# Eighteen groups of transposes in a three-stage fp32 kernel go by 16-bit halves and a transposing DMA instead of by TensorE

## Chip, cores and metric

One core of one Trainium2 chip runs the whole program. The metric is the device time of one execution in microseconds (us), the median of several executions. Before the change it is 501.43 us (three executions, 501.25 to 501.67).

## What is computed

The reference is a chain of three layers on activations of 2 batches x 768 tokens x 512 features, all in fp32:

```python
x = attention(q, k, v)                 # 8 heads of 64, a band of 96 keys and 8 global keys
xt = x.transpose(0, 2, 1)              # first mixer
h = np.maximum(xt @ w_tok1, 0.0) @ w_tok2
u = x + h.transpose(0, 2, 1)
x = u + np.maximum(u @ w_ch1, 0.0) @ w_ch2
theta = x @ w_theta                    # second mixer
zr, zi = x * np.cos(theta), x * np.sin(theta)
y = einsum('ts,bsd->btd', w_tok_r, zr) + einsum('ts,bsd->btd', w_tok_i, zi)
u = x + y
out = u + np.maximum(u @ w_ch, 0.0)
```

The weights arrive as 64-bit floats and are turned into fp32 on the chip.

## The kernel before, in words

**Numbers.** An fp32 matrix product is made of three products of shorter numbers: each operand is split into a high part (hi) and the rest (lo), and `mm3` (line 90) issues hi x hi, hi x lo and lo x hi. ScalarE (ACT) writes hi, VectorE (DVE) or GpSimd (POOL) writes lo = value - hi. `evac_split` (line 704) does that with a result of TensorE (PE) in PSUM.

**Layout.** `x[b]` holds a batch by rows: 6 blocks `s` of 128 tokens on the partitions, 512 features along a partition. A product over features needs the features on the partitions, so each block has to be turned. `turn_rows` (line 775) does that: four PE transposes of 128x128 (line 779) into a PSUM tile, then `evac_split`, so ACT writes hi and DVE lo, both from PSUM. It is called for 24 groups: six `ut` of batch 0, six `ut` of batch 1 (operands of the channel product of the first mixer, kept in `ut[b]`), and twelve `xt`, one for each of the 12 blocks of both batches (operands of `theta` in the second mixer).

**Stages.** Attention of both batches, with the token mixing of batch 0 woven in, takes until about 115 us. `token_mix2` (line 985) does the rows of batch 1 and turns three of its blocks; the other three are turned in the first steps of `channel_mix` (line 996). That has 24 steps (b, k) of 12 per batch. In a step `up` of the step after is issued (8 times 3 products of 512 and of 256 columns into two PSUM banks with the tag "t"; `evac_split` gives the tile `g`), then `down` of the step itself (18 products, tile `h2`). In the steps of batch 1 a small dictionary, `plan`, puts the beginning of the second mixer between `up` and `down`: `pb.turn`, `pb.theta` and `pb.rotate` of the first blocks.

**Second mixer.** `PhaseB.run` (line 1241) goes through 12 steps, one for each block i = (b, s). In step i it issues, in this order: `mix(i, 0)` (24 products of 256 columns), `rotate(i + 1)`, `turn(i + 3)`, `theta(i + 2)`, `mix(i, 1)`, one tick, `mix(i, 2)` (12 products of 512 columns each), and in the first four steps a second tick. From step 7 on parts of the last product (`last`, tile `v`) are put between.
- `theta` (line 1088): 12 products on PE, then five DVE instructions (lines 1105 to 1113) and three of ACT (lines 1116 to 1118) for sine and cosine. `w` for blocks 0 and 1 lies in the pool `tp`, for the others in the pool of `g`.
- `rotate` (line 1129): two DVE products (line 1136), two ACT copies (hi, line 1137), two POOL subtractions (lo, line 1139), and one POOL addition (line 1143) that writes the turned block back into `x`. `z` is what `mix` of the next step reads.
- `turn` (line 1082): `turn_rows` into one of four `xt` tiles, three of the pool `xt` and one in a part of a `z` tile.

**Weights.** Weights are converted by jobs, which run a phase at each tick (`tick`, line 181): load (DMA issued by SyncE, SP), `job_scale` (two ACT), `job_join` (two DVE, lines 145 and 148, and one POOL addition, line 149), `job_high` (one ACT, line 157), `job_low` (one DVE, line 160). One job begins at each tick at most, so several are under way in different phases. In `channel_mix` of batch 0 there are two ticks a step, in that of batch 1 one in `up` and one after `down` where k is not in `plan`.

**What sets the order.** The order is written out by hand. Every engine takes its instructions in the order in which the program issues them, and SP its DMAs as well; an instruction that waits holds back those behind it on its engine.

Of the kernel before, what the change touches and what calls it, by code (L numbers as in the profile page):

```python
# [15 lines left out]
F32 = mybir.dt.float32  # L16
F32R = mybir.dt.float32r
I32 = mybir.dt.int32
U16 = mybir.dt.uint16
AF = mybir.ActivationFunctionType  # L20
ALU = mybir.AluOpType
# [4 lines left out]
P = 128  # L26
NS = S // P
NHP = H // 2
E = H * D
NE = E // P  # L30
# [3 lines left out]
NF = DCH // P  # L34
# [12 lines left out]
LAG = 3  # L47
# [13 lines left out]
def f(ap):  # L61
    return ap.bitcast(F32)


def r(ap):
    return ap.bitcast(F32R)
# [17 lines left out]
class Build:  # L84
# [326 lines left out]
    def attention_band(self, pairs_pool, first, h1):  # L411
# [6 lines left out]
        with tc.tile_pool(name="au", bufs=2) as up, tc.tile_pool(name="aa", bufs=2) as ap:  # L418
# [142 lines left out]
            for u in range(N + 2):  # L561
# [22 lines left out]
                if not turned:  # L584
                    between()
                self.run_steps(
                    turn(u - 1, start and u < N - 4, between) if turned else [],
                    values(u - 2) if 0 <= u - 2 < N else [],
                )
# [180 lines left out]
    def turn_row(self, tag, b, s):  # L770
        h, s0 = divmod(s * P, E)
        hi, lo = (t[h][:, :, s0 : s0 + P] for t in self.ut[b])
        self.turn_rows(tag, self.x[b][:, s, :], r(hi), r(lo), "ut_%d_%d" % (b, s))

    def turn_rows(self, tag, src, hi, lo, name):

        pt = self.ps.tile([P, NE, P], F32, name=name, tag=tag)
        for d in range(NE):
            self.nc.tensor.transpose(pt[:, d, :], src[:, d * P : (d + 1) * P], self.ident)  # L779
        self.evac_split(hi, lo, pt)  # L780
# [192 lines left out]
    def moe(self, es, a8s, w12p, h1):  # L973
        tc = self.tc
        ws = es.enter_context(tc.tile_pool(name="ws", bufs=1, side="right"))
        self.moe_jobs(ws, w12p)
        self.prefetch()
        pend = self.token_mix2(h1)
        a8s.close()
        gp = es.enter_context(tc.tile_pool(name="g", bufs=2, side="right"))  # L980
        xtp = es.enter_context(tc.tile_pool(name="xt", bufs=3, side="right"))
        tp = es.enter_context(tc.tile_pool(name="tb", bufs=1, side="right"))
        self.channel_mix(gp, PhaseB(self, xtp, tp, gp), pend)

    def token_mix2(self, h1):
        pend = []
        for s in range(NS):
            self.token_row("acc", h1, 1, s)
            pend.append(s)
            if len(pend) > LAG:  # L990
                self.turn_row("t", 1, pend.pop(0))
            if s % 2:
                self.tick()
        return pend

    def channel_mix(self, gp, pb, pend):
        nc = self.nc
        steps = [(b, k) for b in range(B) for k in range(NF)]
        ho = {}

        def up(b, k):
            self.need(self.wc_job[k, 0])
            c1 = self.wc[k][0]
            uth, utl = self.ut[b]
            g = gp.tile([P, 2, S], F32R, name="g_%d_%d" % (b, k), tag="g")
            for h, hs in enumerate((slice(0, E), slice(E, S))):
                ps = self.ps.tile([P, hs.stop - hs.start], F32, name="gp_%d_%d_%d" % (b, k, h), tag="t")
                self.mm3(
                    ps,
                    [  # L1010
                        ((r(c1[0][:, d]), r(c1[1][:, d])), (r(uth[h][:, d]), r(utl[h][:, d])))
                        for d in range(NE)
                    ],
                )
                self.evac_split(g[:, 0, hs], g[:, 1, hs], ps, relu=True)
                if pend:
                    self.turn_row("acc", 1, pend.pop(0))
                if b == 0 or h == 1:
                    self.tick()
            return g  # L1020

        def down(b, k, g):
            self.need(self.wc_job[k, 1])
            c2 = self.wc[k][1]
            if k == 0:
                ho[b] = [
                    self.ps.tile([P, E], F32, name="h2_%d_%d" % (b, s), tag="acc") for s in range(NS)
                ]
            for s in range(NS):
                cs = slice(s * P, (s + 1) * P)  # L1030
                self.mm3(
                    ho[b][s],
                    [((g[:, 0, cs], g[:, 1, cs]), (r(c2[0]), r(c2[1])))],
                    first=k == 0,
                    last=k == NF - 1,
                )
                if k == NF - 1:
                    x = self.x[b][:, s, :]
                    nc.vector.tensor_tensor(out=x, in0=ho[b][s], in1=x, op=ALU.add)

        g = up(*steps[0])
        plan = {4: [(pb.turn, 0)], 5: [(pb.theta, 0)], 6: [(pb.rotate, 0), (pb.turn, 1)],
                7: [(pb.theta, 1)], 9: [(pb.turn, 2)]}
        for i, (b, k) in enumerate(steps):
            nxt = up(*steps[i + 1]) if i + 1 < len(steps) else None
            if b == 1:
                for act, n in plan.get(k, ()):
                    act(n)
            down(b, k, g)
            if b == 1 and k < NF - 1 and k not in plan:  # L1050
                self.tick()
            if (b, k) == (0, NF - 2) or b == 1:
                self.gate += 1
            g = nxt
        pb.run()


class PhaseB:
# [10 lines left out]
        self.todo = [(b, s) for b in range(B) for s in range(NS)]  # L1069
        self.xt, self.z, self.y, self.u3 = {}, {}, {}, {}  # L1070

    def xtbuf(self, i):
        j = i % 4
        if j not in self.xtile:
            if j < 3:
                self.xtile[j] = self.xtp.tile([P, 2, NE, P], F32, name="xt%d" % j, tag="xt")
            else:
                t = self.ztile[1][:, 4:6]
                self.xtile[j] = t.rearrange("p l (d x) -> p l d x", d=NE)
        return self.xtile[j]  # L1080

    def turn(self, i):
        b, s = self.todo[i]
        t = self.xt[i] = self.xtbuf(i)
        x = self.k.x[b][:, s, :]
        self.k.turn_rows("t", x, r(t[:, 0]), r(t[:, 1]), "xt_%d_%dp" % (b, s))

    def theta(self, i):
        K, nc = self.k, self.k.nc
# [151 lines left out]
    def run(self):  # L1241
        K = self.k
        n = len(self.todo)
        TA, TB = self.TA, self.TB
        ends = []
        for b in range(B):
            ends += [(b, 0, (0, 1), 0, TB), (b, 0, (2, 3), 0, TB)]
            ends += [(b, 1, (d,), 0, TA) for d in range(NE)]
        ends[-1:] = [(1, 1, (NE - 1,), c, c + TB) for c in range(0, TA, TB)]
        for i, (b, s) in enumerate(self.todo):  # L1250
            self.mix(i, 0)
            if i + 1 < n:
                self.rotate(i + 1)
            if i + 3 < n:
                self.turn(i + 3)
            if i + 2 < n:
                self.theta(i + 2)
            if b == 1 and s in (0, NS - 1):
                self.last_split(s // (NS - 1), 0)
            self.mix(i, 1)  # L1260
            if b == 1 and s > 0:
                self.last(*ends[s - 1])
            if b == 1 and s == 2:
                self.last_split(0, 1)
            K.tick()
            self.mix(i, 2)
            if i < 4:
                K.tick()
        self.last_split(1, 1)
        for end in ends[NS - 1 :]:  # L1270
            self.last(*end)
# [54 lines left out]
```

## Time and profile before

| | |
|---|---|
| median of 3 executions | 501.43 us |
| the profiled execution | 501.55 us, its span 499.8 us |
| PE busy | 494.2 us (99%) |
| DVE busy | 309.0 us (62%) |
| ACT busy | 235.7 us (47%) |
| POOL busy | 163.5 us (33%) |
| TensorE clock granted | 1.0 of full speed in all 40 slices |
| DMA | 45.93 MB, mean 92 GB/s |

The span runs from the first to the last instruction; the 1.75 us between it and the time of the execution lie around it. The duration that the profile gives for a matmul includes its way through the pipeline, so that durations of neighbours overlap; what a matmul costs PE is read from the starts, or from the chain of work that ended last, where the pieces of PE stand end to end.

### The profile page before, as it was taken

The page shows a single profiled execution, that of the slowest core. Times are in us where ns is not written, and L with a number is a line of the kernel's source. Part 1 is how long each engine was busy: PE and PEld are TensorE (multiplying, and loading weights), DVE is VectorE, ACT ScalarE, POOL GpSimd, SP SyncE. Part 2 cuts the span into 40 slices and gives each one's busy share as a digit, 9 for nine tenths or more (in the row PEclk, how much of TensorE's full clock was granted, in tenths as well). Part 3 has the DMA queues.
Part 4 walks back from the last instruction along what each step waited for, and adds up shares of the span by engine and source line. Part 5 has one row for each costly group of instructions (what it writes and reads, how often), then busy time and mean ns, then how long its engine had stood idle before and what let it go on. Part 6 is the DMA issues. An engine that isn't in the chain of part 4 may idle for free.

```text
span 499.8 us, 7723 instructions
## 1 busy us (share of the span) xinstructions
PE 494.2 (99%) x2908; PEld 420.2 (84%) x2908; DVE 309.0 (62%) x671; ACT 235.7 (47%) x458; POOL 163.5 (33%) x175
## 2 busy tenths in 40 slices
PE   9999999999999999999999999999999999999997
PEld 4888878887888888888888888888888889888896
DVE  4788878836876675206573566387888785451342
ACT  6888778714755454112554444445555434232010
POOL 7355444410342323001332151244555543333000
PEclk9999999999999999999999999999999999999999
DMA  6697764201453443002343122222210000000012
GB/s 200 202 266 246 229 215 141 87 2 50 142 159 127 134 126 114 0 1 55 119 129 121 42 54 73 85 85 65 84 64 1 1 1 0 22 22 22 21 66 104
DMA packets 30013, 45.93 MB, mean 92 GB/s; under 512 B 1936, under 2 KB 20880, under 8 KB 29968
## 3 DMA queue, kind: packets, MB, share of 16 engines
q1 hardware_dynamic: 29968, 45.36, 29.7%
q8 instruction: 25, 0.41, 0.3%
q14 instruction: 20, 0.16, 0.1%
HBM read 42.21 MB, written 3.15 MB: 91 GB/s over the span
## 4 chain that ended last, share of the span: by engine, by line
PE 98%; ACT 1%; issue 0%; DVE 0%; DVEq 0%
PE gp L96 20%; PE y L96 20%; PE h L96 20%; PE th L96 7%; PE v L96 7%; PE mm L96 7%; PE o L406 6%; PE s L437 5%; PE t L484 5%; PE warm L330 1%; PE ut L779 1%; PE xt_0p L779 0%; PE xt_2p L779 0%; PE xt_1p L779 0%; ACT e L578 0%; PE xt_4p L779 0%
## 5 line engine op out<-in xcount | busy, mean ns | idle before, releaser
L149 POOL TENSOR_TENSOR cvt<-cvt,cvs 128x512 int32<-128x512 int32 (+1 forms) x57 | 75.8, 1330 | 217.5 <-DVE cvt L148 171.2
L96 PE MATMUL h<-wc,g 128*128 128x512 f32 x432 | 102.1, 390 | 0.0
L96 PE MATMUL gp<-xh,wc 128*128 128x512 f32 (+1 forms) x384 | 97.6, 336 | 0.0
L96 PEld LDWEIGHTS h<-wc,g 128*128 128x128 f32 x432 | 79.6, 188 | 15.4
L708 DVE SCALAR_TENSOR_TENSOR g<-gp,g 128x512 fp32r<-128x512 f32 (+1 forms) x48 | 26.7, 557 | 83.9 <-ACT g L706 83.9
L96 PEld LDWEIGHTS gp<-xh,wc 128*128 128x128 f32 x384 | 67.2, 189 | 8.6 <-DVE xl L712 0.2
L96 PE MATMUL gp<-xl,wc 128*128 128x512 f32 (+1 forms) x192 | 64.3, 335 | 0.0
L706 ACT ACTIVATE g<-gp 128x512 fp32r<-128x512 f32 (+1 forms) x48 | 23.5, 490 | 70.5 <-PE gp L96 70.5
L96 PE MATMUL y<-wri,z 128*128 128x256 f32 (+1 forms) x288 | 51.9, 335 | 0.0
L96 PE MATMUL y<-wri,s 128*128 128x256 f32 (+1 forms) x288 | 51.8, 335 | 0.0
L96 PEld LDWEIGHTS y<-wri,s 128*128 128x128 f32 x288 | 44.7, 189 | 5.9
L96 PEld LDWEIGHTS y<-wri,z 128*128 128x128 f32 x288 | 44.6, 188 | 6.0
L484 PE MATMUL t<-ident,e 128*128 128x128 f32 x176 | 48.0, 285 | 0.4 <-ACT at L496 0.4
L145 DVE SCALAR_TENSOR_TENSOR cvs<-cvt,cvs 128x512 int32<-128x512 int32 (+1 forms) x57 | 44.3, 777 | 0.0
L96 PEld LDWEIGHTS gp<-xl,wc 128*128 128x128 f32 x192 | 36.0, 188 | 4.5
L484 PEld LDWEIGHTS t<-ident,e 128*128 128x128 f32 x176 | 31.7, 184 | 8.1 <-issue 2.0
L450 DVE CUSTOM_DVE_ANT_0 e<-s,base 128x256 f32<-128x256 f32 (+1 forms) x96 | 32.8, 398 | 8.6 <-PE s L437 7.9
L139 ACT ACTIVATE cvt<-raw 128x512 f32<-128x512 f32 (+1 forms) x57 | 37.2, 653 | 2.0 <-issue 2.0
L140 ACT ACTIVATE cvs<-raw 128x512 int32<-128x512 uint16 (+1 forms) x57 | 37.3, 654 | 0.0
L1116 ACT ACTIVATE w<-w 128x512 f32<-128x512 f32 x12 | 7.6, 633 | 56.9 <-DVE w L1113 56.9
L406 PE MATMUL o<-v,at 128*128 128x65 f32 x192 | 32.3, 252 | 0.0
L406 PEld LDWEIGHTS o<-v,at 128*128 128x128 f32 x192 | 29.8, 196 | 0.0
(136 smaller groups left out, 812.9 us busy)
## 6 DMA issues: line engine op xcount, KB each, us to landing
raw<-w_ch SPq DMA_DIRECT2D x28, 512.0 KB, 3.6
raw<-w_tok SPq DMA_DIRECT2D x21, 512.0 KB, 3.6
k<-k SPq DMA_DIRECT2D x7, 480.0 KB, 5.5
v<-v SPq DMA_DIRECT2D x8, 384.0 KB, 3.9
out<-o SPq DMA_DIRECT2D x11, 256.0 KB, 2.0
q<-q SPq DMA_DIRECT2D x7, 384.0 KB, 4.9
raw<-w_theta SPq DMA_DIRECT2D x4, 512.0 KB, 3.6
a<-v SPq DMA_DIRECT2D x8, 240.0 KB, 4.7
```

The source lines that it names most:

```text
L96: self.nc.tensor.matmul(out, lhsT=a, rhs=b, start=first and i == 0, stop=last and i == n - 1)
L139: nc.scalar.activation(out=f(t), in_=f(top), func=AF.Copy, scale=2.0**-111)
L140: nc.scalar.activation(out=s, in_=nxt, func=AF.Copy, scale=2.0**-13)
L145: nc.vector.scalar_tensor_tensor(out=s, in0=t, scalar=-(1 << 31), in1=s, op0=ALU.bitwise_and, op1=ALU.bitwise_or)
L149: nc.gpsimd.tensor_tensor(out=t, in0=t, in1=s, op=ALU.add)
L406: self.nc.tensor.matmul(po[:, j * OW : j * OW + D + 1], lhsT=at, rhs=v[:, j * (D + 1) : (j + 1) * (D + 1)], start=first, stop=last,)
L437: nc.tensor.matmul(ps[j][:, ii, c0:], lhsT=t["q"][pj, i * P : (i + 1) * P], rhs=kf[pj, i * KW - P + c0 : i * KW + P], start=True, stop=True,)
L450: nc.vector.tensor_tensor_reduce(out=e, in0=ps[j][:, ii, c0:], in1=self.base[2 * hp + j][min(i, 1)], op0=ALU.add, op1=ALU.min, scale=-SCAL ...
L484: nc.tensor.transpose(pt[:, ii, c, :], e[j][:, ii, c * P : (c + 1) * P], self.ident)
L706: nc.scalar.activation(out=hi, in_=ps, func=AF.Relu if relu else AF.Copy)
L708: nc.vector.scalar_tensor_tensor(out=lo, in0=ps, scalar=0.0, in1=f(hi), op0=ALU.max, op1=ALU.subtract)
L1116: nc.scalar.activation(out=a, in_=t, func=AF.Abs)
```

## The change

All groups of transposes but the six of batch 0 leave PE. A block of `x` (128 partitions x 512 fp32) is seen as 1024 16-bit halves per partition. `halves_out` copies them so that all lower halves come first and then all upper halves, and SP issues one transposing DMA from SBUF to SBUF (eight blocks of 128x128 halves). `halves_join` copies the turned halves back into their pairs, which gives the turned fp32 block. `halves_split` writes hi (ACT) and lo (DVE), both from SBUF.

For the six blocks of `ut[1]` the two copies are on POOL, in steps k = 2 to 9 of batch 0 of `channel_mix`, issued between `up` and `down`: a block goes out in step s + 2, is joined in step s + 3 and split in step s + 4. For the twelve `xt` blocks the two copies are on ACT; the first four go out in steps of `plan` and the others in `run`, where a step now issues `mix(i, 0)`, `rotate(i + 1)`, `turn_in(i + 3)`, `turn_out(i + 4)`, `theta(i + 2)` and so on. Blocks going out share one tile ("cut") with one buffer; there are three `xt` tiles, the third in the place of `w` of blocks 0 and 1. Steps k = 4 and k = 9 of batch 1 get a tick that they did not have.

```diff
+    def halves_out(self, src, t, copy):
+        a = t[:, 1].rearrange("p d x -> p (d x)").bitcast(U16)
+        b = t[:, 0].rearrange("p d x -> p (d x)").bitcast(U16)
+        copy(
+            out=a.rearrange("p (w n) -> p w n", w=2),
+            in_=src.bitcast(U16).rearrange("p (n w) -> p w n", w=2),
+        )
+        self.nc.sync.dma_start_transpose(out=b.rearrange("p (m x) -> p m x", x=P), in_=a)
+    def halves_join(self, t, copy):
+        b = t[:, 0].rearrange("p d x -> p (d x)").bitcast(U16)
+        c = t[:, 1].rearrange("p d x -> p (d x)").bitcast(U16)
+        copy(out=c.rearrange("p (n w) -> p w n", w=2), in_=b.rearrange("p (w n) -> p w n", w=2))
+    def halves_split(self, t, hi, lo):
+        self.nc.scalar.copy(out=hi, in_=t[:, 1])
+        self.nc.vector.tensor_tensor(out=lo, in0=t[:, 1], in1=f(hi), op=ALU.subtract)
...
-        xtp = es.enter_context(tc.tile_pool(name="xt", bufs=3, side="right"))
+        xtp = es.enter_context(tc.tile_pool(name="xt", bufs=1, side="right"))
...
     def token_mix2(self, h1):
-        pend = []
         for s in range(NS):
             self.token_row("acc", h1, 1, s)
-            pend.append(s)
-            if len(pend) > LAG:
-                self.turn_row("t", 1, pend.pop(0))
             if s % 2:
                 self.tick()
-        return pend
+    def columns_out(self, pb, s):
+        t = self.turning[s] = pb.scratch("ut_%d" % s, ("cut", "xt0", "xt1")[s % 3])
+        self.halves_out(self.x[1][:, s, :], t, self.nc.gpsimd.tensor_copy)
+    def columns_split(self, s):
+        h, s0 = divmod(s * P, E)
+        hi, lo = (u[h][:, :, s0 : s0 + P] for u in self.ut[1])
+        self.halves_split(self.turning.pop(s), r(hi), r(lo))
...
-                if pend:
-                    self.turn_row("acc", 1, pend.pop(0))
...
-        plan = {4: [(pb.turn, 0)], 5: [(pb.theta, 0)], 6: [(pb.rotate, 0), (pb.turn, 1)],
-                7: [(pb.theta, 1)], 9: [(pb.turn, 2)]}
+        self.turning = {}
+        plan = {2: [(pb.turn_out, 0)], 3: [(pb.turn_in, 0), (pb.turn_out, 1)], 4: [(pb.turn_in, 1)],
+                5: [(pb.theta, 0)], 6: [(pb.rotate, 0), (pb.turn_out, 2)], 7: [(pb.theta, 1)],
+                8: [(pb.turn_in, 2)], 9: [(pb.turn_out, 3)]}
         for i, (b, k) in enumerate(steps):
             nxt = up(*steps[i + 1]) if i + 1 < len(steps) else None
+            if b == 0:
+                if 0 <= k - 4 < NS:
+                    self.columns_split(k - 4)
+                if 0 <= k - 3 < NS:
+                    self.halves_join(self.turning[k - 3], nc.gpsimd.tensor_copy)
+                if 0 <= k - 2 < NS:
+                    self.columns_out(pb, k - 2)
...
-            if b == 1 and k < NF - 1 and k not in plan:
+            if b == 1 and k < NF - 1 and k not in (5, 6, 7):
                 self.tick()
...
-    def xtbuf(self, i):
...
-    def turn(self, i):
...
+    def scratch(self, n, tag="cut"):
+        return self.xtp.tile([P, 2, NE, P], F32, name="cut_" + n, tag=tag, bufs=1)
+    def turn_out(self, i):
+        b, s = self.todo[i]
+        t = self.cut = self.scratch("xt_%d_%d" % (b, s))
+        self.k.halves_out(self.k.x[b][:, s, :], t, self.k.nc.scalar.copy)
+    def turn_in(self, i):
+        K = self.k
+        j = (2, 1, 0)[i % 3] if i > 2 else i % 2
         if j not in self.xtile:
+            pool, tag = (self.tp, "t") if j == 2 else (self.xtp, "xt%d" % j)
+            self.xtile[j] = pool.tile([P, 2, NE, P], F32, name="xt%d" % j, tag=tag)
+        t = self.xt[i] = self.xtile[j]
+        K.halves_join(self.cut, K.nc.scalar.copy)
+        K.halves_split(self.cut, r(t[:, 0]), r(t[:, 1]))
...
             if i + 3 < n:
-                self.turn(i + 3)
+                self.turn_in(i + 3)
+            if i + 4 < n:
+                self.turn_out(i + 4)
             if i + 2 < n:
                 self.theta(i + 2)
```

## Rows read from the trace of the kernel before

**Rows 1.** The page: the chain that ended last, shares of the span by engine.

```profile
PE 98%; ACT 1%; issue 0%; DVE 0%; DVEq 0%
```

**Rows 2.** The chain that ended last, in order of time: start us, us, what.

```profile
266.76 0.66 PE xt_0p L779 x4
...
335.28 0.44 PE xt_3p L779 x4
335.71 2.77 PE th L96 x12
...
444.24 2.72 PE th L96 x12
```

**Rows 3.** PE in order of time: start us, us, line and operation, idle before.

```profile
128.34 0.60 PE L779 MATMUL ut<-ident,x 128*128 128x128 f32 x4
128.70 0.37 PE L96 MATMUL gp<-xh,wc 128*128 128x256 f32 x1
```

**Rows 4.** POOL in order of time, steps 3 and 4: lo parts of z, one x.

```profile
373.93 3.00 POOL L1139 TENSOR_TENSOR s<-w,s 128x512 fp32r<-128x512 f32 x2
376.88 1.30 POOL L1143 TENSOR_TENSOR x<-xt 128x512 f32<-128x512 f32 x1
...
386.84 3.01 POOL L1139 TENSOR_TENSOR z<-w,z 128x512 fp32r<-128x512 f32 x2
```

**Rows 5.** PE in order of time: mix part 0 of steps 4 and 5.

```profile
378.18 2.99 PE L96 MATMUL y<-wri,s 128*128 128x256 f32 x24
...
389.65 3.02 PE L96 MATMUL y<-wri,z 128*128 128x256 f32 x24
```

**Rows 6.** DVE in order of time, second mixer, with idle time and its releaser.

```profile
363.39 0.68 DVE L1105 TENSOR_SCALAR w<-th 128x512 f32<-128x512 f32 x1
...
372.13 2.38 DVE L1136 TENSOR_TENSOR w<-x,w 128x512 f32<-128x512 f32 x2
375.69 0.69 DVE L712 TENSOR_TENSOR xt<-xt_0p,xt 128x512 fp32r<-128x512 f32 x1 [1.18 <-ACT xt L706]
376.30 0.68 DVE L1105 TENSOR_SCALAR w<-th 128x512 f32<-128x512 f32 x1
377.02 1.44 DVE L1108 TENSOR_SCALAR w<-w 128x512 f32<-128x512 f32 x1
...
399.33 0.68 DVE L1105 TENSOR_SCALAR w<-th 128x512 f32<-128x512 f32 x1
405.69 1.28 DVE L1136 TENSOR_TENSOR w<-x,w 128x512 f32<-128x512 f32 x2
408.76 0.68 DVE L1105 TENSOR_SCALAR w<-th 128x512 f32<-128x512 f32 x1
```

**Rows 7.** ACT in order of time, step 3 of the second mixer.

```profile
374.55 0.62 ACT L1137 CAST s<-w 128x512 fp32r<-128x512 f32 x1 [1.02 <-DVE w L1136]
375.07 0.59 ACT L706 ACTIVATE xt<-xt_0p 128x512 fp32r<-128x512 f32 x1
```

**Rows 8.** Groups of instructions by line and shape: count, busy us, mean ns.

```profile
L779 PE MATMUL ut<-ident,x 128*128 128x128 f32 x48 | 7.0, 272 | 0.0
L379 POOL TENSOR_SCALAR xh<-x 128x256 fp32r<-128x256 f32 x24 | 11.3, 472 | 29.5 <-DVE x L399 29.5
L1204 ACT CAST u<-x 128x1024 fp32r<-128x1024 f32 x2 | 2.0, 1040 | 0.0
L145 DVE SCALAR_TENSOR_TENSOR cvs<-cvt,cvs 128x512 int32<-128x512 int32 x53 | 41.7, 787 | 0.0
```

**Rows 9.** POOL in order of time, one step of channel_mix, batch 0.

```profile
156.57 1.29 POOL L149 TENSOR_TENSOR cvt<-cvt,cvs 128x512 int32<-128x512 int32 x1 [1.76 <-DVE cvt L148]
161.74 1.29 POOL L149 TENSOR_TENSOR cvt<-cvt,cvs 128x512 int32<-128x512 int32 x1 [3.88 <-DVE cvt L148]
```

**Rows 10.** DMA issues: KB each, median us from issue to landing.

```profile
out<-o SPq DMA_DIRECT2D x11, 256.0 KB, 2.0
raw<-w_tok SPq DMA_DIRECT2D x4, 384.0 KB, 7.3
```

More of the change, by code (lines that the diff above doesn't have):

```diff
@@ L977, in moe, with channel_mix @@
         self.prefetch()
-        pend = self.token_mix2(h1)
+        self.token_mix2(h1)
         a8s.close()
         gp = es.enter_context(tc.tile_pool(name="g", bufs=2, side="right"))
-        xtp = es.enter_context(tc.tile_pool(name="xt", bufs=3, side="right"))
+        xtp = es.enter_context(tc.tile_pool(name="xt", bufs=1, side="right"))
         tp = es.enter_context(tc.tile_pool(name="tb", bufs=1, side="right"))
-        self.channel_mix(gp, PhaseB(self, xtp, tp, gp), pend)
+        self.channel_mix(gp, PhaseB(self, xtp, tp, gp))
     def token_mix2(self, h1):
-        pend = []
         for s in range(NS):
             self.token_row("acc", h1, 1, s)
-            pend.append(s)
-            if len(pend) > LAG:
-                self.turn_row("t", 1, pend.pop(0))
             if s % 2:
                 self.tick()
-        return pend
-    def channel_mix(self, gp, pb, pend):
+    def columns_out(self, pb, s):
[5 more added lines that the diff above has]
+        self.halves_split(self.turning.pop(s), r(hi), r(lo))
+    def channel_mix(self, gp, pb):
         nc = self.nc
@@ L1070, in __init__ @@
         self.xt, self.z, self.y, self.u3 = {}, {}, {}, {}
-    def xtbuf(self, i):
-        j = i % 4
-        if j not in self.xtile:
[L1075 to L1080, printed above, removed]
-    def turn(self, i):
[L1083 to L1086, printed above, removed]
+    def scratch(self, n, tag="cut"):
[7 more added lines that the diff above has]
+        j = (2, 1, 0)[i % 3] if i > 2 else i % 2
+        if j not in self.xtile:
+            pool, tag = (self.tp, "t") if j == 2 else (self.xtp, "xt%d" % j)
[3 more added lines that the diff above has]
+        K.halves_split(self.cut, r(t[:, 0]), r(t[:, 1]))
     def theta(self, i):
```

## The prediction

> **What bounds the kernel now.** I read the chain of work that ended last first. TensorE holds 98% of it [rows 1], so any time taken from PE's queue is gained, as long as no other engine takes its place. The chain in order of time tells what PE pays for a group of four transposes: 0.66 us in the steps of batch 1 of the channel product, 0.44 us in the second mixer [rows 2]. The starts in PE's timeline say the same of `ut`: 128.70 - 128.34 = 0.36 us [rows 3].
>
> Then I looked for the engine that comes next, by asking when `z` is ready and when `mix` wants it. Step 4: POOL ends at 373.93 + 3.00 = 376.93 [rows 4], PE begins at 378.18 [rows 5], 1.25 us to spare. Step 5: 386.84 + 3.01 = 389.85 against 389.65, nothing to spare; PE's 24 products took 3.02 us instead of 2.99, for the lo parts come third. The reason is DVE: from one `theta` to the next its queue takes 376.30 - 363.39 = 12.91 us where two ticks' jobs stand in a step [rows 6], while PE's step takes 389.65 - 378.18 = 11.47 us [rows 5]. DVE falls behind by 1.44 us a step and just reaches step 5 when the jobs run out; without them its turn is 408.76 - 399.33 = 9.43 us [rows 6]. So the second mixer is bound by PE with DVE close behind it, and that decides what the change keeps.
>
> **The sum, part by part.**
>
> *Transposes that leave PE.* Six `ut`: 6 x 0.36 = 2.2 us [rows 3]. Three `xt` in channel steps: 3 x 0.66 = 2.0 us; the part over 0.44 there is a wait for a PSUM bank of the tag "t", which goes too, since `down` needs none. Nine in `run`: 9 x 0.44, and `theta` behind them takes 2.77 instead of 2.72 us [rows 2], so 9 x 0.49 = 4.4 us. Together 8.6 us.
>
> The mean duration of one `ut` transpose is 272 ns in the groups [rows 8], and four of them begin within 0.36 us [rows 3], so I take the starts. The Trainium skill, page "TensorE: Matmul & The Clock Gate", Part 4, gives a transpose 390 ns alone and about 275 ns in a kernel. The row's duration agrees with the latter. Were that what PE pays, 72 transposes would be 72 x 0.275 = 19.8 us and the time 485 us; by the starts it is not.
>
> *Batch 0 of the channel product.* A step (8.2 us) gets two POOL copies of 1024 halves, one ACT copy, one DVE subtraction, one DMA. No row shows a copy of halves on POOL. From the nearest rows: one with a single input takes 472 ns for 256 elements [rows 8], so 1.3 to 1.9 us for 1024 by the share that is fixed; one with two inputs 1.29 us for 512 [rows 9], 2.6 us. I take 1.5, a single input. POOL's idle time in a step is 1.76 + 3.88 = 5.64 us [rows 9]: 3.0 us fit, and 5.2 just fit. Cost nothing, covered by POOL waiting for DVE. If the cover is gone, the additions of line 149 come late, ACT's line 157 behind them, and so the evacuation of `g`. Weights are finished three ticks, 1.5 steps, ahead of their use, which absorbs a few us. `ut` of block 5 is split in step 9 and read from step 11's `up` on.
>
> *Batch 1's channel steps.* Four copies out and three joins on ACT, each near 1.04 us (1024 elements, [rows 8]): 7 us over eight steps of 8.2 us, with ACT at less than half. Nothing, covered by ACT waiting for PE. The two added ticks move two jobs forward, out of `run`.
>
> *The DMA.* No transposing DMA is in the trace. Bounds by rows: 256 KB out land in 2.0 us, the slowest loads, 384 KB, in 7.3 us [rows 10]; I take 4, since it queues behind loads of weights. SP issues it behind loads whose buffers are released by earlier work, so it starts when the copy out ends. In `run` it has the rest of the step: a step less join, hi, lo and copy out (1.04 + 0.6 + 0.7 + 1.04 = 3.4), 11.0 - 3.4 = 7.6 us. Nothing within the bounds.
>
> *The turn in `run`.* Here it costs. Before, ACT writes hi right behind its second copy of `z` (375.07, [rows 7]) and DVE waits 1.18 us for it [rows 6]. Now the join stands before hi: about 1.04 us more. lo would begin at 375.07 + 1.04 + 0.6 = 376.7 instead of 375.69. Its source was PSUM and is now SBUF, so it has two inputs in SBUF, and such an instruction is held while POOL works: the two products of line 1136 take 2.38 us beside POOL and 1.28 without, and line 1108 ends at 377.02 + 1.44 = 378.46, just behind POOL's addition (376.88 + 1.30 = 378.18) [rows 4, 6]. lo arrives near the end of the second subtraction (376.93). If it gets in before the addition, it ends near 377.5, line 1108 then finds POOL done, and the turn is 0.25 us longer. If the addition goes first, lo ends near 378.75, and the turn is 1.4 us longer. I take 0.9, the middle, since lo arrives within 0.2 us of the edge. ACT's copy out waits for lo and then runs beside `theta`'s 4 us on DVE. In step 0 hi also waits for `w`, whose place the third tile takes; `theta` waits for PE there anyway, I estimate 0.3 us.
>
> *What is late next.* PE's step is 0.49 us shorter, DVE's turn 0.9 longer. `z` of step 4: 1.25 - 4 x 0.49 - (0.3 + 2 x 0.9) + 0.3 (the lo parts come third) = -2.5 us. `z` of step 5: -0.2 - 5 x 0.49 - (0.3 + 3 x 0.9) + 0.3, and + 1.9 for the job that is gone from the step before (line 145's 0.79 [rows 8], and products that no longer meet POOL, 2.38 - 1.28): -3.4 us. So PE waits 2.5 us in step 4 and 0.9 more in step 5. With 0.25 it is 1.5 us in all, with 1.4 it is 5.0. After that a turn without jobs is 9.43 + 1.4 at most, under 10.98, and nothing more is lost.
>
> *Sum.* 501.55 - 8.6 + 3.4 = 496.35 us for the profiled execution, which lies 0.12 above the median: **496.2 us**.
>
> **Rivals.**
> 1. *All hidden.* lo finds its gap, and the two jobs moved forward relieve the early steps. For it: DVE has 9.43 us turns later. Against it: nothing is to spare in step 5 now. 501.4 - 8.6 = 492.8 us. Chance 0.14.
> 2. *DVE's turn grows by more than 1.4 us.* ACT's strided copies or the wait for the copy out are longer than 1.04 us; then turns without jobs also exceed PE's 10.98 us, and DVE bounds the second mixer. At 2 us: -0.2 - 2.45 - 6.3 + 0.3 + 1.9 = 6.8 us lost: 499.6 us. For it: no row shows ACT reading or writing every second half at this width. Against it: a turn without jobs has 1.5 us to spare. Chance 0.18.
> 3. *POOL is too slow in batch 0.* At 2.6 us a copy, and DVE held meanwhile, the joins of weights and the two copies follow each other in about 10.9 us against 8.2 over six steps, 16 us, less some 12 of lead: 4 us, with the 3.4: 500 us, up to 503. Against it: single inputs. Chance 0.08.
> 4. *The transposing DMA is slow* (other side). Its blocks go one after another. Place: the join in `run`, in front of `theta`'s ACT work and of lo on DVE. It decides from about 7.6 us: each us over that is paid in about six steps of 11 us. A transposition as slow as the slowest load, behind a load of half that, takes 7.3 + 3.6 = 10.9 us: 6 x 3.3 = 20 less 3 to spare, 501.4 - 8.6 + 17 = 510 us. Against it: 256 KB in 2.0 us [rows 10] and idle queues after the last loads. Chance 0.10. The Trainium skill, page "VectorE: DVE Perf Modes", "The three transpose paths", gives 1309 ns for one 128x128 block by the DMA's crossbar. Eight blocks in a row would be 10.5 us, near this case; no run here shows it yet.
>
> **How the numbers follow.** My case has 0.50, 494.4 to 498 us by its bounds. A difference under 0.2% (1 us) can't be told from none here. Faster: my case, rival 1, most of rival 2 and a little of rival 3: 0.82. Same: ends of rivals 2 and 3, 0.07. Slower: rival 4 and an end of rival 3, 0.11. The range 492.4 to 500.8 takes in rivals 1 and 2 and leaves out rival 4 and most of rival 3.
>
> **What would show it.** Right: no transposes on PE after 121 us; the first `mix` of steps 4 and 5 preceded by PE idle that POOL's line 1139 ends, 3 us in all; lo before 1105 of DVE beginning 1 us later after the products; `theta`'s turn near 13.8 us in steps 1 and 2. Wrong: ACT's join waiting for a DMA (rival 4), POOL without idle time before 200 us (rival 3), PE idle in steps 6 to 11 (rival 2), none at all (rival 1), or PE waiting in the channel steps, which I cost at nothing.

## The result, and the profile after

497.38 us, median of four executions (496.91 to 497.50), against 501.43 of four as well: a ratio of 0.9917, 95% interval 0.9900 to 0.9934. The forecast was 496.2 us, range 492.4 to 500.8. The profiled execution took 497.50 us with a span of 495.7 us, 4.1 us less than before. Line numbers above 775 have moved: the copy out is 779, the transposing DMA 783, the join 789, hi and lo of a turned block 792 and 793, `theta` 1139 to 1152, `rotate` 1170 to 1177; in some of the runs below they lie a few lines off these.

The page of the changed kernel: busy time, the granted clock by slices, the chain by engine.

```profile
PE 486.2 (98%) x2836; PEld 413.8 (83%) x2836; DVE 312.6 (63%) x671; ACT 264.8 (53%) x482; POOL 180.8 (36%) x187
PEclk9999999999999999999999999999998999999999
PE 84%; DVE 7%; ACT 4%; DMA 2%; POOL 1%; SPq 1%; issue 1%; DVEq 0%; ACTq 0%; POOLq 0%
```

PE still has most of the chain [rows 1], but DVE, ACT and POOL now have parts of it, and one slice shows a lower clock. Where this lies is seen in PE's timeline of the second mixer (start, duration, idle before and what ended it), the first part of `mix` in steps 1 to 5 and `theta` of step 4:

```profile
338.64 2.99 PE L96 MATMUL y<-wri,z 128*128 128x256 f32 x24
...
349.63 2.99 PE L96 MATMUL y<-wri,s 128*128 128x256 f32 x24
...
360.62 3.15 PE L96 MATMUL y<-wri,z 128*128 128x256 f32 x24
...
373.46 0.50 PE L96 MATMUL y<-wri,s 128*128 128x256 f32 x2 [1.52 <-ACT s L1171]
375.17 4.38 PE L96 MATMUL y<-wri,s 128*128 128x256 f32 x22 [1.20 <-POOL s L1173]
379.38 2.93 PE L96 MATMUL th<-s,xt 128*128 128x512 f32 x12
...
387.58 2.99 PE L96 MATMUL y<-wri,z 128*128 128x256 f32 x24
```

A step takes 349.63 - 338.64 = 10.99 us instead of 11.47 [rows 5]. Step 4 was due at 360.62 + 10.99 = 371.61, which is 378.18 - 371.61 = 6.6 us earlier than before [rows 5]. It then waits for the hi and the lo parts of `z`, and its 24 products end 4.9 us late: `theta` begins at 379.38, due at 371.61 + 2.83 = 374.44. No later step waits for `z`. The five groups of transposes still to come then give 5 x 0.49 = 2.4 us: 6.6 + 2.4 = 9.0 gained, 4.9 given back, 4.1 left.

DVE in step 2 and its neighbours, with the idle time before an instruction and what ended it:

```profile
348.40 0.68 DVE L1139 TENSOR_SCALAR w<-th 128x512 f32<-128x512 f32 x1
...
356.13 2.39 DVE L1170 TENSOR_TENSOR w<-x,w 128x512 f32<-128x512 f32 x2
361.19 1.53 DVE L793 TENSOR_TENSOR xt<-cut_xt,xt 128x512 fp32r<-128x512 f32 x1 [2.67 <-ACT xt L792]
362.65 0.68 DVE L1139 TENSOR_SCALAR w<-th 128x512 f32<-128x512 f32 x1
363.36 0.43 DVE L1142 TENSOR_SCALAR w<-w 128x512 f32<-128x512 f32 x1
```

ACT in the same step:

```profile
358.55 0.62 ACT L1171 CAST z<-w 128x512 fp32r<-128x512 f32 x1 [1.03 <-DVE w L1170]
359.08 1.36 ACT L789 COPY cut_xt<-cut_xt 128x1024 uint16<-128x1024 uint16 x1
360.47 0.62 ACT L792 CAST xt<-cut_xt 128x512 fp32r<-128x512 f32 x1
```

POOL in steps 2 to 4:

```profile
357.93 3.00 POOL L1173 TENSOR_TENSOR z<-w,z 128x512 fp32r<-128x512 f32 x2
360.90 1.27 POOL L1177 TENSOR_TENSOR x<-xt 128x512 f32<-128x512 f32 x1
...
372.17 2.94 POOL L1173 TENSOR_TENSOR s<-w,s 128x512 fp32r<-128x512 f32 x2
...
384.97 2.55 POOL L1173 TENSOR_TENSOR z<-w,z 128x512 fp32r<-128x512 f32 x2 [2.00 <-issue]
```

DVE's turn from `theta` to `theta` is 362.65 - 348.40 = 14.25 us, 1.34 us more than before [rows 6]. Read together: ACT writes the second hi of `z`, then the join (1.36 us), then hi of the turned block. lo reaches the head of DVE's queue at 361.19, 0.29 us after POOL has begun its addition (360.90), and takes 1.53 us instead of 0.69 [rows 6]: it ends 0.55 us behind the addition's end (362.17). Line 1142, which stood behind that addition before (1.44 us, [rows 6]), now takes 0.43 us. The Trainium skill, page "SBUF — State Buffer", section "SBUF: two separate sides", says that a DVE instruction with two SBUF inputs and a GpSimd instruction that reads SBUF take one port pair by turns, for a whole instruction. This timeline agrees: of lo's 1.53 us, 0.98 pass beside the addition, and it ends 0.55 us behind it.

`z` of step 4 is finished by POOL at 372.17 + 2.94 = 375.11, 3.5 us after PE wanted to begin.

The new copies (groups by line and shape) and the transposing DMAs (SP's issues, median us from issue to landing):

```profile
L789 ACT COPY cut_xt<-cut_xt 128x1024 uint16<-128x1024 uint16 x12 | 16.3, 1362 | 0.0
L779 ACT COPY cut_xt<-x 128x1024 uint16<-128x1024 uint16 x12 | 12.5, 1046 | 10.0 <-DVE xt L793 10.0
L789 POOL COPY cut_ut<-cut_ut 128x1024 uint16<-128x1024 uint16 x6 | 9.6, 1594 | 2.9 <-DMA cut_ut<-cut_ut 2.9
L779 POOL COPY cut_ut<-x 128x1024 uint16<-128x1024 uint16 x6 | 7.6, 1262 | 0.0
```

```profile
cut_xt<-cut_xt SPq DMA_TRANSPOSE x12, 2.7
cut_ut<-cut_ut SPq DMA_TRANSPOSE x6, 2.7
```

### The profile page after: what moved, and what is told of

It reads as the page before. It is cut to its first block, busy times and chain, and to the rows that moved or that the text cites. A ratio compares the mean times of both kernels' runs of the same rounds, so it can differ in the third digit from the quotient of the medians.

```text
span 495.7 us, 7653 instructions
## 1 busy us (share of the span) xinstructions
PE 486.2 (98%) x2836; PEld 413.8 (83%) x2836; DVE 312.6 (63%) x671; ACT 264.8 (53%) x482; POOL 180.8 (36%) x187
## 4 chain that ended last, share of the span: by engine, by line
PE 84%; DVE 7%; ACT 4%; DMA 2%; POOL 1%; SPq 1%; issue 1%; DVEq 0%; ACTq 0%; POOLq 0%
PE gp L96 20%; PE h L96 18%; PE y L96 14%; PE v L96 7%; PE mm L96 7%; PE o L406 6%; PE th L96 5%; PE t L484 4%; PE s L437 4%; DMA k<-k 1%; DVE w L1170 1%; DMA q<-q 1%; DVE cvs L145 1%; DVE xt L793 1%; DVE x L1061 1%
## 5 line engine op out<-in xcount | busy, mean ns | idle before, releaser
L96 PE MATMUL y<-wri,s 128*128 128x256 f32 (+1 forms) x288 | 53.7, 344 | 2.7 <-ACT s L1171 1.5
L96 PEld LDWEIGHTS y<-wri,s 128*128 128x128 f32 x288 | 46.2, 196 | 9.2 <-ACT s L1171 1.9
L96 PE MATMUL th<-s,xt 128*128 128x512 f32 x144 | 35.0, 392 | 0.0
L96 PEld LDWEIGHTS th<-s,xt 128*128 128x128 f32 x144 | 26.3, 189 | 5.2 <-DVE g L708 0.4
```

The source lines that it names most:

```text
L96: self.nc.tensor.matmul(out, lhsT=a, rhs=b, start=first and i == 0, stop=last and i == n - 1)
```

## Experiments

The question was where the 4.9 us come from. My theory: DVE's turn in `run` is too long as long as two ticks' jobs stand in it, since the join precedes hi and lo meets POOL. Rivals: the `ut` part (POOL in batch 0), lo's second SBUF operand alone, the ticks alone. Each kernel was run beside the kernel before, whose median was 501.3 to 501.7 us in the four sets.

**The two parts apart (e1, e2).** e1 keeps `turn_rows` and the old `plan` for `xt`; e2 keeps it for `ut`:

```diff
+                self.turn(i + 3)                        # e1, in run
-                self.turn_in(i + 3)
-                self.turn_out(i + 4)
...
+            if len(self.pend) > LAG:                    # e2, in token_mix2 and up
+                self.turn_row("t", 1, self.pend.pop(0))
```

> Only the six ut groups go by halves (POOL copies); the twelve xt groups stay on TensorE as before, with the ticks of before. Theory (POOL and the DMA of batch 0 are hidden; what the change gives back is lost in the second mixer): 501.4 less six groups, 2.2 to 2.6 us, gives 498.9 to 499.3 us, and PE's first mix of steps 4 and 5 as before. Rival (POOL's copies hold DVE and the weights come late): 500 to 502 us, with PE idle in the channel steps.

Measured: 498.74 us, ratio 0.9944 (0.9927 to 0.9960), 2.6 us faster than before, and PE does not wait for `z`. Against what its expectation says, e1 keeps the two added ticks (k = 4 and 9). They don't show here, since PE waits for no engine in the second mixer, neither in e1 nor before.

> Only the twelve xt groups go by halves (ACT copies); the six ut groups stay on TensorE. Theory: the wait in step 4 of the second mixer (4.8 us in the changed kernel, some 2 of them at a lower granted clock) is there in full, so 497.4 plus the six groups, 2.3 us: 499.7 us, 498 if the clock does not fall. DVE's turn again near 14.25 us. Rival (the wait comes from ut's part, or from PE arriving earlier by the ut groups): wait under 2 us, 497 us or less.

Measured: 499.58 us, ratio 0.9966 (0.9953 to 0.9978). PE in step 4 of e2:

```profile
375.50 0.50 PE L96 MATMUL y<-wri,s 128*128 128x256 f32 x2 [1.54 <-ACT s L1170]
377.21 4.00 PE L96 MATMUL y<-wri,s 128*128 128x256 f32 x22 [1.20 <-POOL s L1172]
```

The same wait at the same place. The parts add, within the intervals: 2.6 + 1.7 = 4.3 us against 4.1. So batch 0's part is hidden whole, and all that is given back belongs to the `xt` part.

**The join (e3, e6).** e3 leaves the join out in `run`; e6 only moves it:

```diff
-        K.halves_join(self.cut, K.nc.scalar.copy)       # e3: not for i > 2, hi and lo from x
...
+            if i + 3 < n:                               # e6, in run, ahead of rotate(i + 1)
+                K.halves_join(self.cut, K.nc.scalar.copy)
```

> As the changed kernel, without the nine copies of line 789 on ACT in run; hi and lo are taken from the block of x as it stands, so xt is not turned there. Theory (the join in front of hi delays lo, and with it DVE's turn): lo begins some 1.3 us earlier, the turn is 12.9 to 13.2 us instead of 14.25, the wait in step 4 under 1.2 us and no fall of the clock: 493 to 494.5 us. Rival (the turn is longer only because lo now reads two operands in SBUF, and the join fits into a gap): the turn stays over 13.8 us and the time over 496 us.

Measured: 495.02 us, ratio 0.9871 (0.9855 to 0.9888). The turn is 13.37 us (from the starts of lo, 345.14 and 358.51). lo, from DVE's timeline, and PE's waits in steps 4 and 5, from PE's:

```profile
358.51 1.69 DVE L793 TENSOR_TENSOR xt<-x,xt 128x512 fp32r<-128x512 f32 x1 [1.28 <-ACT xt L792]
```

```profile
373.06 2.79 PE L96 MATMUL y<-wri,s 128*128 128x256 f32 x22 [1.22 <-POOL s L1179]
...
385.03 2.78 PE L96 MATMUL y<-wri,z 128*128 128x256 f32 x22 [0.77 <-POOL z L1179]
```

Without the join lo is issued earlier, and then stands behind a subtraction of POOL (1.69 us). So the join is the larger part of the longer turn (0.88 of 1.34 us). The rest goes with lo's second SBUF operand: beside a subtraction of POOL lo took 0.69 us while its source was in PSUM [rows 4, 6], and 1.69 here. I had expected a little more, a turn of 12.9 to 13.2 us and 493 to 494.5 us.

> As the changed kernel, with the join of a step of run issued ahead of rotate, so that ACT does it while it waits for DVE's products. Theory (the join in front of hi lengthens the turn): hi and lo come about 1 us earlier, the turn falls from 14.25 to about 13.2 us, but the lo parts of z come up to 1 us later; the wait in step 4 shrinks by 1 us or so: 495.5 to 496.5 us. Rival (the wait follows from the jobs alone): no change, 497.4 us; slower if z is what suffers.

Measured: 495.39 us, ratio 0.9872 (0.9856 to 0.9889), 2.0 us better than the changed kernel by an order of issue alone. The turn is 358.76 - 345.27 = 13.49 us, by lo's starts. Who kept PE waiting in e6 (us in total, times, longest):

```profile
PE y L96 <- POOL s L1174: 1.4, 1, 1.4
PE y L96 <- POOL z L1174: 1.3, 1, 1.3
```

The wait is now spread over steps 4 and 5, and the granted clock stays at 1.00 throughout.

**POOL's addition (e4).** It is issued behind the first tick in steps 0 to 4:

```diff
-        nc.gpsimd.tensor_tensor(out=x, in0=whole(xt[:, 0]), in1=whole(xt[:, 1]), op=ALU.add)
...
             K.tick()
+            if i < 5:
+                self.restore(i + 1)                     # the same addition
```

> As the changed kernel, with POOL's addition that writes x back issued behind the first tick of steps 0 to 4 instead of right behind the two subtractions. Theory (lo loses the race against that addition and waits for it): lo takes 0.7 us instead of 1.53, the turn falls to about 13.5 us, the wait in step 4 to 1 to 2 us: 495 to 496 us. Rival (lo is slow by itself from SBUF): lo stays at 1.5 us and the time at 497.4 us. A third way: the addition now meets the two products of DVE and costs there what it saves: turn 14.2 us, 497.4 us.

Measured: 498.15 us, ratio 0.9940 (0.9923 to 0.9956). lo, two `theta` and line 145 of the second tick in DVE's timeline, then the addition in POOL's:

```profile
347.72 0.68 DVE L1139 TENSOR_SCALAR w<-th 128x512 f32<-128x512 f32 x1
...
354.38 1.75 DVE L145 SCALAR_TENSOR_TENSOR cvs<-cvt,cvs 128x512 int32<-128x512 int32 x1
...
361.55 0.69 DVE L793 TENSOR_TENSOR xt<-cut_xt,xt 128x512 fp32r<-128x512 f32 x1 [2.65 <-ACT xt L792]
362.15 0.68 DVE L1139 TENSOR_SCALAR w<-th 128x512 f32<-128x512 f32 x1
```

```profile
353.84 1.75 POOL L1183 TENSOR_TENSOR x<-xt 128x512 f32<-128x512 f32 x1
```

lo takes 0.69 us now, so its 1.53 were the meeting with the addition. But the turn is 362.15 - 347.72 = 14.43 us: the addition now meets line 145 of the second tick of the same step, which takes 1.75 us instead of 0.69. My expectation that the turn would shrink failed, and the third way that it named came true, with the jobs in the place of the two products. Moving a meeting is not removing it.

**The jobs (e5, e7, e8).** e5 gives the changed kernel ticks in k = 5, 6 and 7 too, e7 is e5 with e6, e8 is the kernel before with a tick in every one of these steps:

```diff
-            if b == 1 and k < NF - 1 and k not in (5, 6, 7):
+            if b == 1 and k < NF - 1:
```

> As the changed kernel, with a tick in steps k = 5, 6 and 7 of batch 1 of the channel product too, so that three more jobs' phases lie ahead of the second mixer. Theory (DVE falls behind PE only while two jobs' phases stand in its turn): steps 0 to 2 have six instructions of jobs less on DVE, 5 us or so, z of step 4 comes in time, PE does not wait in step 4 and the clock stays: 497.4 - 4.8 = 492.6 us. Rival (the turn is too long even without the jobs): PE still waits over 1 us in steps 4 or 5, 494.5 us or more. Also possible: DVE is late at the beginning of the second mixer instead.

> e5 and e6 together. Theory: nothing is left to wait for after e5, so as e5, 492.6 us within 0.4. If e5 left a wait, it is smaller here by up to 1 us.

> The kernel before, with a tick in every step of batch 1 of the channel product (k = 4, 5, 6, 7 and 9 too). Theory: the kernel before has no wait of PE in the second mixer, so moving jobs forward gives nothing: 501.3 us, no difference. Rival (the ticks by themselves make the kernel faster): 499 us or less.

Measured: e5 497.71 us, ratio 0.9926 (0.9909 to 0.9942); e7 496.00, 0.9883 (0.9867 to 0.9900); e8 503.61, 1.0043 (1.0026 to 1.0059). PE's waits in the profiled executions of e5 and of e8:

```profile
PE th L96 <- DVE g L708: 2.6, 1, 2.6
PE y L96 <- POOL s L1173: 1.1, 1, 1.1
```

```profile
PE th L96 <- DVE g L708: 1.1, 1, 1.1
PE xt_1p L779 <- DVE g L708: 1.1, 1, 1.1
```

All three went otherwise than I expected; for e5 both figures of the rival came out (PE waits over 1 us in step 4, and the time is over 494.5 us). The wait in the second mixer does shrink (1.1 us in e5, 0.7 in e7), but the ticks put new work in front of the evacuation of `g`, and PE waits 2.6 us (2.5 in e7) for a PSUM bank in step 7. The profiled execution of e5 is the fastest of its four, 496.12 us; two others took 498.3 us at a mean granted clock of 0.996 to 0.997, so these two waits do not account for the whole median. In e8 the same ticks cost 2.0 us, with 2.2 us of such waits, and have nothing to gain. The jobs can be moved, but not into all three of those steps.

**The jobs the other way (e9 to e12).** e9 moves the last jobs back, into turns that have room; e10 is e9 with e6, e11 is e10 with a tick in k = 7, e12 is the kernel before with e9's edit:

```diff
-            if i < 4:
+            if i < 2:
                 K.tick()
```

> As the changed kernel, with the second tick of a step of run only in steps 0 and 1 instead of 0 to 3, so that the jobs of the last weights go to steps 2 to 6, one tick each. Theory (DVE falls behind only in turns with two ticks, and turns with one or none have room): step 2's turn falls from 14.2 to 10.5 us, z of step 4 comes 3.7 us earlier and in time, PE waits under 0.5 us in steps 4 to 6: 493 us within 0.5. Rival (the longer turn is too long even with one tick, so the wait moves to steps 5 and 6): 494.5 us or more.

> e9 with the join issued ahead of rotate as in e6 (495.4 us, PE's wait there 2.9 us). Theory: no wait left, all of what PE gave up is gained: 492.5 us within 0.5, as e9 or better by up to 0.5. Rival: z's lo parts, which e6 moves back, now bound steps 4 and 5: 494 us.

> e10 with one more tick, in step k = 7 of batch 1 of the channel product alone (e5, with ticks in 5, 6 and 7, made PE wait 2.6 us there for the evacuation of g). Theory (it is the ticks in k = 5 and 6, behind the first sine and beside the first rotate, that held g): no wait there, and as e10 within 0.4. Rival: any tick there holds g: slower than e10 by 1 us or more.

> The kernel before, with the second tick of a step of run only in steps 0 and 1, as e9 does it to the changed kernel. Theory: PE does not wait for z in the kernel before, so fewer ticks give nothing there: 501.4 us, no difference; the 4.5 us that e9 gained belong to the change's wait. Rival (the ticks cost PE time in either kernel): 499 us or less. Also possible: slower, if weights come late.

Measured: e9 492.88 us, ratio 0.9825 (0.9808 to 0.9841); e10 493.11, 0.9834 (0.9817 to 0.9850); e11 492.74, 0.9833 (0.9816 to 0.9849). In e9 PE's wait for `z` and DVE's turn in step 3 (372.74 - 362.45 = 10.29 us):

```profile
PE y L96 <- POOL s L1173: 0.4, 1, 0.4
```

```profile
362.45 0.68 DVE L1139 TENSOR_SCALAR w<-th 128x512 f32<-128x512 f32 x1
...
372.13 0.69 DVE L793 TENSOR_TENSOR xt<-cut_xt,xt 128x512 fp32r<-128x512 f32 x1 [2.65 <-ACT xt L792]
372.74 0.68 DVE L1139 TENSOR_SCALAR w<-th 128x512 f32<-128x512 f32 x1
```

One tick fewer in two steps brings the whole gain: 8.8 us against the 9.0 that PE gave up, with the same transposing DMAs, copies and halves. Neither the join ahead nor another early tick adds to that within the intervals, since little is left to wait for: 0.4 us for `z` in e9, 0.7 in e10, none in e11. In e11 the tick in k = 7 alone makes no wait for `g` either, as expected. This settles the cause: DVE's turns with two ticks. e9 does not price the jobs and the meeting apart, though: in the turn shown lo gets ahead of POOL's addition again (0.69 us). e9 changes one number of the changed kernel and is faster than both kernels; no other edit tried is faster than e9 beyond the intervals.

e12 was forecast to change nothing, with late weights named as a possibility, and is slower: 508.93 us, ratio 1.0156 (1.0139 to 1.0173). PE's waits there:

```profile
PE v L96 <- DVE wch L160: 3.3, 1, 3.3
PE v L96 <- ACT wch L157: 1.3, 1, 1.3
```

The last weights come too late: PE waits 4.6 us for them, and the clock granted there falls to 0.50 (426 to 430 us). The changed kernel has two more ticks ahead of `run`, in k = 4 and 9, which I had costed as no more than a relief; the kernel before, without them, cannot spare the ticks that e9 takes away. The changed kernel without these two was not run.

## Why the prediction was right, point by point

- *PE's part.* 8.6 us were forecast, 9.0 measured. e1 prices a transpose at 2.6 / 24 = 0.11 us (0.08 to 0.15 by its interval), so the starts [rows 3] and not the duration of 272 ns [rows 8] were the measure.
- *POOL in batch 0, ACT in batch 1, the DMA: nothing.* Right, by e1. POOL's copies took 1.26 and 1.59 us; I had taken 1.5.
- *The DMA.* 4 us taken, 2.7 measured, in a gap of 7.6. Rival 4 fell. Rival 2 fell too: a turn without jobs takes 10.30 us (line 1139 at 397.72 and at 408.02), under PE's 10.99. The page "VectorE: DVE Perf Modes" of the Trainium skill, with 1309 ns for a block, would make eight in a row 10.5 us, an estimate; here eight take 2.7 us from issue to landing, so the measurement decides against reading it so.
- *The turn in `run`.* The mechanism was right, and both cases that it named bound what came: POOL's addition went ahead of lo, and the turn grew by 1.34 us, near the upper end (1.4), not by the 0.9 that I took. The mis-sized term is the join: 1.36 us, not 1.04. It is the larger part of what put lo 0.29 us behind the beginning of POOL's addition, where the sum had it 0.2 us ahead.
- *What is late next.* Step 4, as forecast; `z` was due with 2.5 us of delay and came 3.2 us late after the allowance of 0.3. The first 1.5 us of PE's wait were ended by ACT's hi and not, as I had named for a sign, by POOL's lo; both come late by DVE's products. With 1.34 in place of 0.9 the same sum gives 1.25 - 1.96 - 2.98 + 0.3 = -3.4, and for step 5 -0.2 - 2.45 - 4.32 + 0.3 + 1.9 = -4.8 us in all, against 4.9 measured. The second part of it did not show as a wait in step 5: PE lost it in step 4 already, by the clock (below). The sum holds no clock, so that it comes within 0.1 us of the measured loss is in part luck.
- *Net.* Gains 0.4 above, losses 1.5 above the forecast: 1.1 to 1.2 us slower than 496.2.

## What to carry to other kernels

Work that leaves the bounding engine is worth what the engine next to it has to spare in that stage: compare, step by step, when a product is ready and when it is wanted, and extend the two lines by what each engine gains and pays. Before adding work to the engine that falls behind, see what else stands in its queue that could as well be done where it has room: here moving two ticks was worth 4.5 us, more than any other single edit. And a copy in front of another engine's input can cost that engine most of its length (here 0.88 of 1.36 us a turn), even on an engine that is idle half the time.

## What the runs showed of the hardware

The granted clock by stretches of the changed kernel, around the wait in step 4 (stretch, its length, busy time and count of PE, PEld, DVE, ACT and POOL, clock, DMA):

```profile
366.00:371.80 5.80, 5.80 (x27) 4.59 (x25) 4.90 (x8) 5.51 (x10) 2.48 (x2) 1.00 0.11 22
371.80:373.50 1.70, 0.18 (x2) 0.04 (x1) 0.95 (x1) 0.71 (x2) 1.70 (x2) 1.00 0.00 0
373.50:375.20 1.70, 0.50 (x3) 0.29 (x3) 0.00 (x0) 1.67 (x2) 1.70 (x3) 1.00 0.00 0
375.20:376.20 1.00, 1.00 (x8) 1.00 (x9) 0.79 (x1) 0.10 (x1) 1.00 (x1) 0.88 0.00 0
376.20:377.20 1.00, 1.00 (x6) 1.00 (x6) 1.00 (x2) 0.26 (x1) 0.16 (x1) 0.50 0.04 8
377.20:378.20 1.00, 1.00 (x7) 1.00 (x6) 0.93 (x3) 0.78 (x1) 0.00 (x0) 0.50 0.00 0
378.20:379.50 1.30, 1.30 (x8) 1.30 (x8) 1.23 (x3) 0.00 (x0) 0.00 (x0) 0.55 0.24 56
379.50:382.00 2.50, 2.50 (x13) 2.03 (x12) 2.00 (x4) 2.06 (x4) 0.32 (x1) 1.00 0.34 76
```

PE, at 2.4 GHz until then, was busy for 0.68 of 3.4 us, took up its work, and was then granted 1.2 GHz from about 376 until shortly before 379.5; the 22 products took 4.38 us, where the same 22 took 2.79 in e3, which had waited 1.22 us in one piece. I had not priced that. It cost little on top: PE began step 5 at 387.58, and 1.6 us earlier it would have waited for `z`, of which POOL wrote the lo parts until 384.97 + 2.55 = 387.52. The four executions agree: 496.91 us in the one with a mean granted clock of 1.00, 497.30 to 497.50 in the three with 0.995 to 0.997.

Which waits are followed by a lower clock is not told by the length of one piece alone. e2 and e4 show the fall as the changed kernel does, after two pieces of 1.2 to 1.7 us with two products between, and e12 after 3.3 us. The waits of 0.4 to 1.4 us of e3, e6 and e9 left no such mark, and neither did the 2.6 us of e5 in one piece (291.47 to 294.03, the clock at 1.00 through it and behind it). What decides it was not tried.

Two copies of the same 1024 halves differ: the one out, 1046 ns on ACT, the join, 1362 ns. They differ in which side steps over every second half; that this is the reason was not tried.
